# The last two of seven pair products deferred into the next stage, the experts' products all plain, and low parts computed on GpSimd

## The chip, the cores and the metric

One core of one Trainium2 chip runs the whole program in one launch. TensorE (PE) does the matmuls; PEld is its loading of weights. VectorE (DVE), ScalarE (ACT) and GpSimd (POOL) do elementwise work; SyncE (SP) and POOL issue DMAs. The metric is the device time of one execution in microseconds (us), a median over runs. Each engine works through its own list of instructions in order, and starts one when the semaphores that it names have been reached.

## The reference

Attention over 2 x 8 heads of 576 x 64, then a mixture of 8 experts, then a dense feed-forward, all float32. What bears on the change is the last two:

```
for e in range(E):                  # 8 experts, d_model 512, d_ff 1024
    h = np.maximum(x @ w1[e], 0.0)
    ye = h @ w2[e]
    out += P[:, e:e + 1] * ye       # P: balanced gates
...
h = x @ w_in                        # d_ff 2048
g = np.maximum(h, 0.0) + np.log1p(np.exp(-np.abs(h)))
return (g @ w_out).astype(np.float32)
```

x has 1152 rows (tokens) of 512.

## The kernel before

Each float32 operand is split into a high part (rounded to the matmul's format, by ACT) and a low part (the operand less its high part, by DVE or POOL); a product is three matmuls: high by high, high by low, low by high. In tile names the last letter, h or l, is that part.

The hidden dimension is worked off in 20 batches x of 512 features: 0 to 15 are the experts' (two each; relu), 16 to 19 the dense layer's (softplus). The rows are two halves g of 576. A batch has a first product (x by w1, tiles `ph`, L502), always as seven products of quarters; for a half g and each of two feature blocks a and b it is p1, p2, p6, p7, p5, p3, p4, six matmuls of 288 columns each, called a **first unit** here (a1, b1, ... b4: 14 to a half).

The second product (hidden by w2, added into `acc`) has two forms. The **plain** one (`downs`, L578) takes 36 **down units** of three matmuls of 512 columns to a batch. The **seven** form (`pairs`, L420), for the batches in `SEVEN` (14, 17, 18, 19), takes for each half seven products of quarters, a11·b11, s3·t3, s2·t2, a22·t4, s1·t1, s4·b22, a12·b21, each as two **pair units** r of six matmuls of 256 columns, and for the 128 rows left over (one row tile, NB) four down units. It has two PSUM banks, one for each r; each bank holds two halves of columns. A pair unit accumulates onto one half of a bank; behind every pair unit DVE adds that half into `acc` (`add_to`, L381; 128x256), and the next unit that accumulates on that half waits for the add.

For the seven form ACT writes the hidden block as plain words (`evict`, tile `hw`), and `h_steps` makes from them the sums s1 to s4 (POOL, L334), their high parts (ACT, L327) and low parts (DVE, L330). `prep_t` makes t1 to t4 from w2 (sums on POOL L256, high parts on ACT L243, low parts `tl` on DVE L245); `prep_b` splits w2's blocks (ACT L226, `w2l` on DVE L228). `prep1` sums and splits the next batch's w1 (POOL L161 to L170, ACT L152, DVE L155). POOL's chain has one scratch tile `xw` for both s and t.

Nothing is reordered by a scheduler: `play` reads a string. `a1` to `b4` issue a first unit, `d` the next second unit, and each such token then lets one step of each waiting helper (`back`, `side`, `bot`) be issued. A **first stage** of x plays the first units of half 1 of x with the second units of half 0; a **second stage** plays the first units of half 0 of x+1 with the second units of half 1; behind batch 19 comes a **last stage** without first units. `E` and `F` (and before `e`) start parts of `h_steps`, `x`/`y` start `prep_b`/`prep_t`.

Of the kernel before, what the change touches and what calls it, by code (L numbers as in the profile page):

```python
# [20 lines left out]
def attention_moe_ffn(ctx, tc, q, k, v, s, w_gate, w1, w2, w_in, w_out, out):  # L21
    nc = tc.nc
# [107 lines left out]
    SEVEN = (NX - 2, NX + 1, NX + 2, NX + 3)  # L130
# [89 lines left out]
    def prep_b(x, n):  # L220

        if x >= NH:
            return
        raw = blocks(x)[n]
        hi, lo = (w2_block(n, z) for z in w2_t)
        nc.scalar.activation(out=hi, in_=raw, func=AF.Copy)  # L226
        yield
        nc.vector.tensor_tensor(out=lo, in0=raw, in1=f(hi), op=ALU.subtract)  # L228
        if n == "21":
            load(x + 1, 2, 1)  # L230
        ready.add((x, "b" + n))
        yield
# [7 lines left out]
    def t_part(x, n, src, part):  # L240
# [3 lines left out]
        else:  # L244
            nc.vector.tensor_tensor(out=l, in0=src, in1=f(h), op=ALU.subtract)  # L245
# [76 lines left out]
    def h_steps(x, g, part):  # L322
# [13 lines left out]
        if part == "e":  # L336
            hold((x, g), (None,))
            sum_("s3", "a11", "a21", ALU.subtract)
            high("a11")
            yield  # L340
            low("a11")
            yield
            last = (x - 1 + g, 1 - g)
            assert not seven(last[0]) or (*last, "done") in ready
            high("s3")
            yield
        elif part == "E":
            high("m")
            high("a22")
            yield  # L350
            low("s3")
            low("m")
            low("a22")
            sum_("s2", "a22", "s3", ALU.subtract)
            yield
            sum_("s1", "a21", "a22", ALU.add)
            yield
            high("a12")
            yield
            low("a12")  # L360
            high("s2")
            yield
            sum_("s4", "a12", "s2", ALU.subtract)
            high("s1")
            yield
            low("s2")
            low("s1")
            hold(None, ((x, g),))
            yield
        else:  # L370
# [3 lines left out]
            yield  # L374

# [13 lines left out]
    def pairs(x, g, middle=None):  # L389
# [16 lines left out]
        for a, b, bank, start, tile_, col, first in (  # L406
# [4 lines left out]
            if a == "s3" and middle is not None:  # L411
                yield from middle
            for r in range(2):
# [9 lines left out]
                if a == "s4" and r:  # L423
                    ready.add((x, g, "done"))
# [61 lines left out]
    class Unit:  # L486
# [32 lines left out]
        def p2(self):  # L519
# [4 lines left out]
            evict(self.x, 5 if seven(self.x) else 0, b, self.p, self.h0)  # L524
# [11 lines left out]
        def p5(self):  # L536
# [5 lines left out]
            evict(self.x, 1, t, self.p + 2, self.h1)  # L542
# [60 lines left out]
    with tc.manual_schedule():  # L603
# [685 lines left out]
        def play(seq, todo, d=None):  # L1289


            for z in seq.split():
# [14 lines left out]
                if z[0] in "eEF":  # L1307
                    g = int(z[1])
                    if seven(x if g else x + (z[0] == "e")):
                        side.append(h_steps(x if g else x + (z[0] == "e"), g, z[0]))  # L1310
# [13 lines left out]
        A7_SEQ = "E0 a1 b1 a2 b2 =0 d d a6 d b6 d d F0 a7 d d b7 =1 d d a5 d b5 d d a3 d b3 e1 a4 d b4"  # L1324
        A7_LAST = "E0 a1 b1 a2 b2 d a6 d d b6 d d F0 a7 d d b7 d d a5 d b5 d a3 d b3 e1 a4 b4 d d"
        B7_SEQ = ("E1 a1 b1 =2 a2 b2 d d d d a6 d d {11} b6 d d {3} F1 a7 d b7 d {2} a5 d b5 d {4} d a3 d {1} d b3 e0 d {22} a4 d b4 d {21}")
        TO_SEVEN = B_SEQ.replace("b2", "b2 y3 y2 y4 y1").replace("b3", "b3 e0")
        B7 = {True: {"11": "x11 x12 y0", "3": "y3", "2": "y2", "4": "y4", "1": "y1", "22": "x22", "21": "x21"},
              False: {"11": "w0 w1", "3": "", "2": "", "4": "", "1": "", "22": "", "21": "w2 w3"}}
# [12 lines left out]
        for x in range(NH):  # L1342
# [8 lines left out]
            if seven(x):  # L1351
                play(A7_SEQ if x + 1 < NH else A7_LAST, products(x, 1), pairs(x, 0))
# [9 lines left out]
            if seven(x):  # L1362
                if x + 1 < NH:
                    seq = B7_SEQ
# [79 lines left out]
```

## Time and profile before

| | |
|---|---|
| median of 3 runs | 1088.13 us (1088.04 to 1088.27) |
| the profiled execution | 1089.59 us, of which 1087.8 are the span of the trace |
| mean granted TensorE clock | 0.996 |
| PE busy | 1056.2 us (97% of the span) |
| DVE, ACT, POOL busy | 799.5, 525.3, 406.1 us |

A busy PE is pipelined: a matmul's duration overlaps the next one's start, so the price of a unit is read from start to start. A gap before a matmul is printed in brackets with what ended it. Stretches are given in us from the start of the span. Batch 13 is plain (742.77 to 790.25), batch 14 seven (790.25 to 839.68); the stages of 17 to 19 go from 942.30 to 1084.15.

### The profile page before, as it was taken

The numbers are of one execution on the slowest core, as the hardware profiler recorded it, in microseconds if no ns is written. First come the engines' busy times: TensorE is split into PE (matmuls) and PEld (weight loads), VectorE is DVE, ScalarE is ACT, GpSimd is POOL, SyncE is SP. The second block draws the span as 40 slices with busy tenths as digits, with TensorE's granted clock in tenths as the row PEclk, the third lists the DMA queues.
The fourth block names the chain that finished last, engine by engine and source line by source line (L and its number), as shares of the span: only waits on it lengthen the run. The fifth ranks groups of instructions, "written<-read, shape, count | busy, mean of one in ns | idle before, by whom it ended". The sixth has DMA issues, their size and how long they took to land.

```text
span 1087.8 us, 18435 instructions
## 1 busy us (share of the span) xinstructions
PE 1056.2 (97%) x6876; PEld 942.5 (87%) x6876; DVE 799.5 (73%) x1725; ACT 525.3 (48%) x1232; POOL 406.1 (37%) x449
## 2 busy tenths in 40 slices
PE   6999999999999999999999999999999999999987
PEld 4777888889888888988888898888899888898987
DVE  5576566667877878787887888775477487678876
ACT  6998544334443433434343343334454365555542
POOL 8885303053342414134241423423262233546321
PEclk9999999999999999999999999999999999999999
DMA  6221111122232222223222231311111011201002
GB/s 195 78 83 55 39 40 39 40 92 96 89 130 88 80 97 98 100 77 124 91 74 98 97 107 68 127 59 39 39 40 59 20 40 39 78 21 59 1 16 73
DMA packets 31538, 78.47 MB, mean 72 GB/s; under 512 B 5856, under 2 KB 13024, under 8 KB 31448
## 3 DMA queue, kind: packets, MB, share of 16 engines
q1 hardware_dynamic: 28704, 68.69, 18.9%
q0 software_dynamic: 2560, 8.39, 2.0%
q8 instruction: 54, 0.88, 0.3%
q14 instruction: 36, 0.29, 0.1%
q10 hardware_dynamic: 184, 0.20, 0.1%
HBM read 65.99 MB, written 10.75 MB: 71 GB/s over the span
## 4 chain that ended last, share of the span: by engine, by line
PE 82%; DVE 10%; ACT 3%; issue 2%; POOL 2%; DMA 0%; POOLq 0%; ACTq 0%; DVEq 0%
PE py L578 36%; PE ph L502 35%; PE py L420 5%; DVE hl L330 2%; PE sc L794 2%; POOL eb L857 1%; PE pv L901 1%; DVE sl L330 1%; PE tr L875 1%; DVE xl L1198 1%; DVE acc L381 1%; DVE xt L1229 1%; DVE ph L523 1%; PE sc L798 1%; DVE w1l L155 1%
## 5 line engine op out<-in xcount | busy, mean ns | idle before, releaser
L502 PE MATMUL ph<-xh,w1h 128*128 128x288 f32 x1120 | 331.7, 296 | 0.3 <-ACT v L510 0.3
L502 PE MATMUL ph<-xh,w1l 128*128 128x288 f32 x1120 | 330.8, 295 | 0.0
L502 PE MATMUL ph<-xl,w1h 128*128 128x288 f32 x1120 | 329.3, 294 | 0.0
L578 PE MATMUL py<-w2h,hh 128*128 128x512 f32 x588 | 233.5, 397 | 1.0 <-DVE acc L590 1.0
L578 PE MATMUL py<-w2l,hh 128*128 128x512 f32 x588 | 232.5, 395 | 0.2 <-POOL w2l L201 0.2
L578 PE MATMUL py<-w2h,hl 128*128 128x512 f32 x588 | 232.4, 395 | 0.0
L502 PEld LDWEIGHTS ph<-xh,w1h 128*128 128x128 f32 x1120 | 210.0, 188 | 18.4 <-ACT v L510 0.5
L502 PEld LDWEIGHTS ph<-xl,w1h 128*128 128x128 f32 x1120 | 210.4, 188 | 16.9
L502 PEld LDWEIGHTS ph<-xh,w1l 128*128 128x128 f32 x1120 | 210.3, 188 | 0.0
L510 ACT ACTIVATE v<-ph 128x288 f32<-128x288 f32 x160 | 64.0, 409 | 187.5 <-PE ph L502 184.8
L469 ACT ACTIVATE hh<-ph 128x288 fp32r<-128x288 f32 x180 | 73.7, 411 | 151.8 <-DVE ph L552 78.2
L578 PEld LDWEIGHTS py<-w2h,hl 128*128 128x128 f32 x588 | 110.5, 188 | 26.5
L201 POOL TENSOR_TENSOR w2l<-raw,w2h 128x512 fp32r<-128x512 f32 x36 | 51.3, 1427 | 215.9 <-ACT w2h L199 215.9
L596 DVE SCALAR_TENSOR_TENSOR acc<-py,gate,acc 128x512 f32<-128x512 f32 x118 | 88.0, 746 | 49.2 <-PE py L578 49.0
L1166 POOL TENSOR_TENSOR cm<-cm,ct 128x512 f32<-128x512 f32 x32 | 45.1, 1408 | 201.5 <-DVE ct L1164 201.5
L578 PEld LDWEIGHTS py<-w2h,hh 128*128 128x128 f32 x588 | 110.4, 188 | 10.5 <-DVE acc L590 1.2
L578 PEld LDWEIGHTS py<-w2l,hh 128*128 128x128 f32 x588 | 110.5, 188 | 10.0 <-POOL w2l L201 0.7
L155 DVE TENSOR_TENSOR w1l<-raw,w1h 128x512 fp32r<-128x512 f32 (+1 forms) x160 | 109.8, 686 | 11.3 <-ACT w1h L152 11.3
L476 DVE SCALAR_TENSOR_TENSOR hl<-ph,hh 128x288 fp32r<-128x288 f32 x180 | 81.2, 453 | 26.7 <-ACT hh L469 25.1
L152 ACT ACTIVATE w1h<-raw 128x512 fp32r<-128x512 f32 (+1 forms) x160 | 91.1, 571 | 0.0
L541 DVE TENSOR_TENSOR t<-ph,v 128x288 f32<-128x288 f32 x80 | 36.4, 455 | 54.5 <-ACT v L510 53.9
L510 ACT ACTIVATE u<-ph 128x288 f32<-128x288 f32 x80 | 32.7, 411 | 55.5 <-PE ph L502 53.4
(246 smaller groups left out, 1779.2 us busy)
## 6 DMA issues: line engine op xcount, KB each, us to landing
raw<-in_w SPq DMA_DIRECT2D x64, 512.0 KB
f<-in_w_in SPq DMA_DIRECT2D x16, 512.0 KB
f<-in_w_out SPq DMA_DIRECT2D x16, 512.0 KB
wd<-cm POOLq DMA_DIRECT2D x32, 256.0 KB, 3.1
raw<-wd SPq DMA_DIRECT2D x16, 512.0 KB
vv<-in_v SPq DMA_DIRECT2D x8, 256.0 KB
out<-acc SPq DMA_DIRECT2D x16, 128.0 KB
qk<-in_k SPq DMA_DIRECT2D x7, 288.0 KB
```

Of the source, the lines that this page charges most:

```text
L152: nc.scalar.activation(out=hi[:, o], in_=t[:, src], func=AF.Copy)
L155: nc.vector.tensor_tensor(out=lo[:, o], in0=t[:, src], in1=f(hi[:, o]), op=ALU.subtract)
L201: (nc.gpsimd if i else nc.vector).tensor_tensor(out=lo, in0=t[:, r], in1=f(hi), op=ALU.subtract)
L420: nc.tensor.matmul(o, u, v, start=(start and c == 0 and n == 0), stop=(c == 1 and n == 2), skip_group_check=True)
L469: nc.scalar.activation(out=hh, in_=z, func=AF.Relu)
L476: nc.vector.scalar_tensor_tensor(out=hl, in0=z, scalar=0.0, in1=f(hh), op0=ALU.max, op1=ALU.subtract)
L502: nc.tensor.matmul(o, u, v, start=(start and c == 0 and n == 0), stop=(c == 1 and n == 2), skip_group_check=True)
L510: nc.scalar.activation(out=t, in_=self.a, func=AF.Copy)
L541: defer(0, lambda: nc.vector.tensor_tensor(out=t, in0=self.c, in1=u4, op=ALU.add))
L578: nc.tensor.matmul(py[t], u, v, start=(k == 0 and n == 0), stop=(k == NF - 1 and n == 2))
L596: nc.vector.scalar_tensor_tensor(out=a, in0=py, scalar=gate_t[0][:, t, e:e + 1], in1=a, op0=ALU.mult, op1=ALU.add)
L1166: nc.gpsimd.tensor_tensor(out=m, in0=m, in1=f(t), op=ALU.add)
```

## The change

Batch 14 leaves `SEVEN`. In the stages of 17 to 19, `h_steps` is no longer begun in the stage before (`e`): `E` holds all but s4. The generator `pairs` gives only its first five products (ten units) in its own stage; the last two (s4·b22 and a12·b21, four units) stay in `d` and are issued at the start of the next stage. The four down units of the tile NB move ahead of the second half's pairs, as before, but behind the deferred four; in the last stage they are played between these. In the first stage of 17, which has nothing deferred, the first pair unit comes behind a6. Of w2's blocks, b22 and b21 are split in the first stage (`X22`, `X21`), no longer in the second. The words of p2 and p5 are written 8 and 4 flushes later (before 5 and 1). The low parts `tl` and `w2l` in `t_part` and `prep_b` go from VectorE to GpSimd.

```
-    SEVEN = (NX - 2, NX + 1, NX + 2, NX + 3)
+    SEVEN = (NX + 1, NX + 2, NX + 3)
...
     def prep_b(x, n):
...
-        nc.vector.tensor_tensor(out=lo, in0=raw, in1=f(hi), op=ALU.subtract)
+        nc.gpsimd.tensor_tensor(out=lo, in0=raw, in1=f(hi), op=ALU.subtract)
...
     def t_part(x, n, src, part):
...
-            nc.vector.tensor_tensor(out=l, in0=src, in1=f(h), op=ALU.subtract)
+            nc.gpsimd.tensor_tensor(out=l, in0=src, in1=f(h), op=ALU.subtract)
...
     def h_steps(x, g, part):
...
-        if part == "e":
-            hold((x, g), (None,))
-            sum_("s3", "a11", "a21", ALU.subtract)
-            high("a11")
-            yield
-            low("a11")
-            yield
-            last = (x - 1 + g, 1 - g)
-            assert not seven(last[0]) or (*last, "done") in ready
-            high("s3")
-            yield
-        elif part == "E":
-            high("m")
-            high("a22")
-            yield
-            low("s3")
-            low("m")
-            low("a22")
-            sum_("s2", "a22", "s3", ALU.subtract)
-            yield
-            sum_("s1", "a21", "a22", ALU.add)
-            yield
-            high("a12")
-            yield
-            low("a12")
-            high("s2")
-            yield
-            sum_("s4", "a12", "s2", ALU.subtract)
-            high("s1")
-            yield
-            low("s2")
-            low("s1")
-            hold(None, ((x, g),))
-            yield
-        else:
+        if part == "F":
+            assert (x, g, "s3 done") in ready
+            return
+        hold((x, g), (None,))
+        sum_("s3", "a11", "a21", ALU.subtract)
+        high("m")
+        yield
+        high("a11")
+        low("m")
+        yield
+        high("a22")
+        low("a11")
+        yield
+        low("a22")
+        yield
+        last = (x - 1 + g, 1 - g)
+        assert not seven(last[0]) or (*last, "s4 done") in ready
+        high("s3")
+        yield
+        low("s3")
+        yield
+        sum_("s2", "a22", "s3", ALU.subtract)
+        yield
+        high("a12")
+        yield
+        sum_("s1", "a21", "a22", ALU.add)
+        yield
+        high("s2")
+        yield
+        low("s2")
+        yield
+        low("a12")
+        high("s1")
+        yield
+        sum_("s4", "a12", "s2", ALU.subtract)
+        low("s1")
+        hold(None, ((x, g),))
+        yield
...
     class Unit:
...
-            evict(self.x, 5 if seven(self.x) else 0, b, self.p, self.h0)
+            evict(self.x, 8 if seven(self.x) else 0, b, self.p, self.h0)
-            evict(self.x, 1, t, self.p + 2, self.h1)
+            evict(self.x, 4 if seven(self.x) else 1, t, self.p + 2, self.h1)
...
         def play(seq, todo, d=None):
...
-                if z[0] in "eEF":
-                    g = int(z[1])
-                    if seven(x if g else x + (z[0] == "e")):
-                        side.append(h_steps(x if g else x + (z[0] == "e"), g, z[0]))
+                if z[0] in "EF":
+                    side.append(h_steps(x, int(z[1]), z[0]))
+                    continue
+                if z[0] == "X":
+                    bot.append(prep_b(x, z[1:]))
...
-        A7_SEQ = "E0 a1 b1 a2 b2 =0 d d a6 d b6 d d F0 a7 d d b7 =1 d d a5 d b5 d d a3 d b3 e1 a4 d b4"
-        A7_LAST = "E0 a1 b1 a2 b2 d a6 d d b6 d d F0 a7 d d b7 d d a5 d b5 d a3 d b3 e1 a4 b4 d d"
-        B7_SEQ = ("E1 a1 b1 =2 a2 b2 d d d d a6 d d {11} b6 d d {3} F1 a7 d b7 d {2} a5 d b5 d {4} d a3 d {1} d b3 e0 d {22} a4 d b4 d {21}")
-        TO_SEVEN = B_SEQ.replace("b2", "b2 y3 y2 y4 y1").replace("b3", "b3 e0")
-        B7 = {True: {"11": "x11 x12 y0", "3": "y3", "2": "y2", "4": "y4", "1": "y1", "22": "x22", "21": "x21"},
-              False: {"11": "w0 w1", "3": "", "2": "", "4": "", "1": "", "22": "", "21": "w2 w3"}}
+        A7_SEQ = ("E0 a1 ~ b1 ~ {22} a2 ~ b2 ~ {21} =0 a6 d b6 d a7 d b7 d F0 =1 a5 d b5 d a3 d b3 d a4 d b4 d")
+        B7_SEQ = ("E1 a1 d b1 d a2 d b2 d =2 a6 d d b6 d d {12} a7 d d {11} b7 d d {3} F1 a5 d b5 d {2} a3 d b3 d {4} a4 d b4 d {1}")
+        TO_SEVEN = B_SEQ.replace("b2", "b2 y3 y2 y4 y1")
+        B7 = {True: {"12": "x12", "11": "x11 y0", "3": "y3", "2": "y2", "4": "y4", "1": "y1"},
+              False: {"12": "", "11": "w0 w1", "3": "", "2": "", "4": "", "1": "d d d d w2 w3"}}
+        A7 = {True: {"~": "d", "{22}": "X22", "{21}": "X21"}, False: {"~": "", "{22}": "", "{21}": ""}}
+        LAST = "E1 d d D d D d D D d d d d F1 " + "d " * 10
...
         for x in range(NH):
...
-                play(A7_SEQ if x + 1 < NH else A7_LAST, products(x, 1), pairs(x, 0))
+                seq = A7_SEQ
+                for k, z in A7[seven(x - 1)].items():
+                    seq = seq.replace(k, z)
+                d = then(d if seven(x - 1) else (), pairs(x, 0))
+                play(seq, products(x, 1), d)
...
+                    d = then(d, downs(x, [(NB,)]), pairs(x, 1))
-                    play(seq, products(x + 1, 0), then(downs(x, [(NB,)]), pairs(x, 1)))
+                    play(seq, products(x + 1, 0), d)
-                    play("E1 n n n n " + "d " * 8 + "F1 " + "d " * 10, {}, pairs(x, 1, downs(x, [(NB,)], "tr")))
+                    middle = downs(x, [(NB,)], "tr")
+                    play(LAST, {"D": lambda: next(middle)}, then(d, pairs(x, 1)))
```

In `pairs` and `h_steps` the flag "done" is now kept for each product ("s3 done", "s4 done").

VectorE at the opening of the first stage of batch 18, before (`sl` and `hl` are low parts of s and of the hidden quarters, `acc` an add behind a pair unit, `ph` an add of the first product):

```order
L381 TENSOR_TENSOR acc<-py,acc 128x256
L330 TENSOR_TENSOR sl<-xw,sh 128x512
L330 TENSOR_TENSOR hl<-hw,hh 128x4x64
L330 TENSOR_TENSOR hl<-hw,hh 128x2x2x128
L228 TENSOR_TENSOR w2l<-raw_10292,w2h 128x2x256
L523 TENSOR_TENSOR ph<-ph,v 128x288 x2
L381 TENSOR_TENSOR acc<-py,acc 128x256
L330 TENSOR_TENSOR hl<-hw,hh 128x2x2x128
L381 TENSOR_TENSOR acc<-py,acc 128x256
L330 TENSOR_TENSOR sl<-xw,sh 128x512
L330 TENSOR_TENSOR hl<-hw,hh 128x2x2x128
L381 TENSOR_TENSOR acc<-py,acc 128x256 x3
```

and after (L384 is L381 of before, L524 is L523):

```order
L330 TENSOR_TENSOR hl<-hw,hh 128x4x64
L330 TENSOR_TENSOR hl<-hw,hh 128x2x2x128
L384 TENSOR_TENSOR acc<-py,acc 128x256
L330 TENSOR_TENSOR hl<-hw,hh 128x2x2x128
L524 TENSOR_TENSOR ph<-ph,v 128x288
L384 TENSOR_TENSOR acc<-py,acc 128x256
L330 TENSOR_TENSOR sl<-xw,sh 128x512
L524 TENSOR_TENSOR ph<-ph,v 128x288
L384 TENSOR_TENSOR acc<-py,acc 128x256 x2
L330 TENSOR_TENSOR sl<-xw,sh 128x512
L384 TENSOR_TENSOR acc<-py,acc 128x256
L330 TENSOR_TENSOR hl<-hw,hh 128x2x2x128 x2
```

The `w2l` is gone. All low parts of the half but s4's now stand in this stage, mostly one between two adds; before, a11's stood in the stage ahead, and s3's, m's and a22's followed each other.

GpSimd in the same stage, before, from the sum for t2 on (`xw<-hw` is s3, `xw<-hw,xw` s2, `hw<-hw` s1, `hw<-hw,xw` s4, `raw` with 128x256 the sums of w1):

```order
L256 TENSOR_TENSOR xw<-raw_10292,raw_10267 128x512
L256 TENSOR_TENSOR xw<-raw_10292,xw 128x512
L334 TENSOR_TENSOR xw<-hw 128x512
L334 TENSOR_TENSOR xw<-hw,xw 128x512
L334 TENSOR_TENSOR hw<-hw 128x2x2x128
L161 TENSOR_TENSOR raw_10624<-raw_10624 128x256
L163 TENSOR_TENSOR raw_10624<-raw_10624 128x256
L334 TENSOR_TENSOR hw<-hw,xw 128x2x2x128
L161 TENSOR_TENSOR raw_10681<-raw_10681 128x256
```

and after, from the low part of t4 on:

```order
L245 TENSOR_TENSOR tl<-xw,th 128x512
L334 TENSOR_TENSOR xw<-hw 128x512
L245 TENSOR_TENSOR tl<-raw_10129,th 128x512
L228 TENSOR_TENSOR w2l<-raw_10154,w2h 128x2x256
L334 TENSOR_TENSOR xw<-hw,xw 128x512
L161 TENSOR_TENSOR raw_10505<-raw_10505 128x256
L334 TENSOR_TENSOR hw<-hw 128x2x2x128
L163 TENSOR_TENSOR raw_10505<-raw_10505 128x256
L228 TENSOR_TENSOR w2l<-raw_10154,w2h 128x2x256
L161 TENSOR_TENSOR raw_10565<-raw_10565 128x256
L163 TENSOR_TENSOR raw_10565<-raw_10565 128x256
L334 TENSOR_TENSOR hw<-hw,xw 128x2x2x128
```

Three low parts, one `tl` and two `w2l`, now stand between s3, s2, s1 and s4, and s4 has all four first sums of w1 ahead of it.

ScalarE in the same stage around s4's high part (`v` is the copy of p5 that the next product on its PSUM tile waits for, `hw` a word of the hidden block), before:

```order
L152 ACTIVATE w1h_10931<-raw_10624 128x512
L458 ACTIVATE hw<-ph 128x288
L152 ACTIVATE w1h_10957<-raw_10681 128x512
L327 ACTIVATE sh<-hw 128x512
L510 ACTIVATE v<-ph 128x288
L152 ACTIVATE w1h_11019<-raw_10624 128x512
L458 ACTIVATE hw<-t_11009 128x288
L510 ACTIVATE v<-ph 128x288
```

and after:

```order
L152 ACTIVATE w1h_10823<-raw_10565 128x512
L511 ACTIVATE v<-ph 128x288
L327 ACTIVATE sh<-hw 128x512
L511 ACTIVATE v<-ph 128x288
L459 ACTIVATE hw<-ph 128x288
L459 ACTIVATE hw<-t_10834 128x288
L459 ACTIVATE hw<-ph 128x288
L152 ACTIVATE w1h_10889<-raw_10505 128x512
L459 ACTIVATE hw<-t_10854 128x288
```

The high part of s4 stands between the copies of a5 and of b5; before, both came behind it.

## Rows read from the trace of the kernel before

**Rows 1.** The page: busy time of each engine, and the chain that ended last.
```profile
PE 1056.2 (97%) x6876; PEld 942.5 (87%) x6876; DVE 799.5 (73%) x1725; ACT 525.3 (48%) x1232; POOL 406.1 (37%) x449
...
PE 82%; DVE 10%; ACT 3%; issue 2%; POOL 2%; DMA 0%; POOLq 0%; ACTq 0%; DVEq 0%
```

**Rows 2.** Stages: length, busy us (count) by engine, granted clock, DMA share, GB/s.
```profile
742.77:790.25 47.48, 47.48 (x279) 42.56 (x277) 25.05 (x47) 18.84 (x45) 15.26 (x15) 1.00 0.13 45
790.25:839.68 49.43, 45.68 (x350) 44.52 (x349) 39.68 (x75) 25.46 (x56) 18.60 (x16) 1.00 0.16 54
942.30:965.61 23.31, 21.55 (x170) 21.14 (x169) 18.36 (x34) 12.80 (x29) 14.70 (x13) 1.00 0.14 46
965.61:993.03 27.42, 24.80 (x182) 23.46 (x181) 23.73 (x39) 15.13 (x34) 11.13 (x8) 1.00 0.11 39
993.03:1015.87 22.84, 21.53 (x170) 21.12 (x169) 18.41 (x36) 12.05 (x28) 13.27 (x12) 1.00 0.14 48
1015.87:1043.29 27.42, 24.78 (x182) 23.47 (x181) 23.74 (x39) 15.15 (x34) 11.13 (x8) 1.00 0.00 1
1043.29:1066.33 23.04, 21.54 (x170) 21.11 (x168) 16.04 (x32) 10.52 (x25) 5.53 (x4) 1.00 0.10 35
1066.33:1084.15 17.82, 15.27 (x98) 14.10 (x96) 13.43 (x23) 3.46 (x7) 3.98 (x3) 0.90 0.20 68
```

**Rows 3.** TensorE in order of time: start, duration, line, tiles; first matmuls of units.
```profile
640.43 0.29 PE L502 MATMUL ph<-xh,w1h 128*128 128x288 f32 x1
...
641.23 0.39 PE L578 MATMUL py<-w2h,hh 128*128 128x512 f32 x1
...
641.93 0.39 PE L578 MATMUL py<-w2h,hh 128*128 128x512 f32 x1
...
954.39 0.28 PE L420 MATMUL py<-th,hh 128*128 128x256 f32 x1
...
955.10 0.29 PE L502 MATMUL ph<-xh,w1h 128*128 128x288 f32 x1
```

**Rows 4.** TensorE's waits in the stages with pairs (in brackets).
```profile
823.24 0.38 PE L420 MATMUL py<-w2h,hh 128*128 128x256 f32 x1 [1.69 <-DVE acc L596]
...
974.61 0.39 PE L420 MATMUL py<-w2h,hh 128*128 128x256 f32 x1 [1.34 <-DVE acc L593]
...
985.52 0.38 PE L420 MATMUL py<-th,hh 128*128 128x256 f32 x1 [1.08 <-DVE acc L381]
...
1075.16 0.36 PE L420 MATMUL py<-th,sh 128*128 128x256 f32 x1 [2.23 <-DVE acc L381]
```

**Rows 5.** VectorE and then GpSimd ahead of the wait at 974.61.
```profile
971.58 0.68 DVE L330 TENSOR_TENSOR sl<-xw,sh 128x512 fp32r<-128x512 f32 x1
972.18 1.78 DVE L330 TENSOR_TENSOR hl<-hw,hh 128x512 fp32r<-128x512 f32 x1
973.88 0.68 DVE L593 TENSOR_TENSOR acc<-py,acc 128x512 f32<-128x512 f32 x1
...
971.73 1.67 POOL L334 TENSOR_TENSOR hw<-hw,xw 128x512 f32<-128x512 f32 x1 [0.96 <-DVE hl L330]
```

**Rows 6.** Groups from 930 to 1065: busy us, mean ns; idle before, and what ended it.
```profile
L381 DVE TENSOR_TENSOR acc<-py,acc 128x256 f32<-128x256 f32 x68 | 27.9, 417 | 11.7 <-PE py L420 11.3
L334 POOL TENSOR_TENSOR hw<-hw,xw 128x512 f32<-128x512 f32 x5 | 8.1, 1616 | 2.6 <-DVE hl L330 2.6
L245 DVE TENSOR_TENSOR tl<-xw,th 128x512 fp32r<-128x512 f32 x7 | 4.8, 687 | 3.2 <-ACT th L243 3.2
L256 POOL TENSOR_TENSOR xw<-raw,xw 128x512 f32<-128x512 f32 x3 | 3.9, 1298 | 8.5 <-DVE tl L245 8.5
L161 POOL TENSOR_TENSOR raw<-raw 128x256 f32<-128x256 f32 x4 | 3.9, 963 | 0.0
```

**Rows 7.** The clock in the last stage, in the columns of the stages.
```profile
1076.70:1080.10 3.40, 3.40 (x18) 3.40 (x17) 1.87 (x4) 0.00 (x0) 0.00 (x0) 0.50 0.11 39
```

**Rows 8.** ScalarE in the second stage of batch 17: a wait for a POOL sum.
```profile
982.56 0.64 ACT L243 ACTIVATE th<-raw 128x512 fp32r<-128x512 f32 x1 [3.65 <-POOL raw L256]
```

More of the change, by code (lines that the diff above doesn't have):

```diff
@@ L387, in add_to, with pairs @@
             nc.sync.dma_start(out=out[t * P:(t + 1) * P, cols], in_=a)
-    def pairs(x, g, middle=None):
+    def pairs(x, g):
         z = h_sets(g)
@@ L410, in pairs @@
                 ("a12", "b21", 1, True, 0, 0, False)):
-            if a == "s3" and middle is not None:
-                yield from middle
             for r in range(2):
@@ L422, in pairs @@
                 flush()
-                if a == "s4" and r:
-                    ready.add((x, g, "done"))
+                if r:
+                    ready.add((x, g, a + " done"))
                 add_to(x, rows_of(g) // P + 2 * r + tile_, d[col], o, first, (tile_, col))
```

## The prediction, made before the changed kernel was run

> **What bounds it now.** I read the page first: PE is busy for 97% of the span and holds 82% of the chain that ended last [rows 1], so the time is PE's work plus PE's waits. The table by stages then tells where the waits are. Batch 13, plain, is 47.48 us long and PE is busy for all of it; the stages with pairs are not full [rows 2]. From start to start a first unit costs 0.80 us (640.43 to 641.23), a down unit 0.70 (to 641.93), a pair unit 0.71 (954.39 to 955.10) [rows 3]. So a plain batch is 28 x 0.80 + 36 x 0.70 = 47.6, as measured. A first stage with pairs would be 14 x 0.80 + 14 x 0.71 = 21.14, a second 14 x 0.80 + 14 x 0.71 + 4 x 0.70 = 23.94, the last 14 x 0.71 + 4 x 0.70 = 12.74. Measured in batches 17 to 19 [rows 2]: 23.31, 27.42, 22.84, 27.42, 23.04, 17.82; over the ideal by 2.17, 3.48, 1.70, 3.48, 1.90 and 5.08, together **17.8 us lost**.
>
> The waits printed before matmuls show what the loss is: nearly always a unit that waits for a DVE add [rows 4]. Ahead of the one at 974.61 DVE does two low parts and only then the add of NB's total, and the second of them takes 1.78 us, because POOL has a sum running from 971.73 to 973.40 [rows 5]; the one ahead of it took 0.68. An add that reads PSUM is not stretched: 417 ns on average [rows 6]. In the last stage two waits of DVE adds end with one of 2.23 us [rows 4], after which the granted clock is 0.5, the 1.2 GHz level, for 3.4 us [rows 7]: half of that, 1.7, is lost again.
>
> **Batch 14.** It had 49.43 us; as a plain batch it should take what batch 13 takes, 47.48 [rows 2]. By parts: 36 x 0.70 - 28 x 0.71 - 4 x 0.70 = 2.5 us more matmul work, against 49.43 - 45.08 = 4.35 us of waits, such as the 1.69 at 823.24 [rows 4]. Gain **1.95**. The cover is PE's own work: DVE is busy for 25.05 of 47.48 us, ACT for 18.84, POOL for 15.26, so the plain form's `hl` and `w2l` are hidden. Without that cover the waits would stay in another form and the batch lose 2.5.
>
> **Batches 17 to 19, PE's work.** The ten or four units only move: the six stages become 18.3, 23.94, 21.14, 23.94, 21.14 and 15.58, again 124.0 in all. What changes is the waits, which I follow by the order of each engine, with the durations DVE 0.69 for a low part and 0.42 for an add, POOL 1.30, or 1.62 where DVE is in its way, 0.96 for a 256-column sum [rows 6], ACT 0.64 for a high part [rows 8].
>
> Behind a pair unit the same bank half is wanted next after 5 us in a first stage (a first unit stands between any two pair units) and after 2.3 us across a stage's border, where it was 0.7 to 2.2. A single low part caught behind POOL (1.78) no longer delays PE there. What remains late:
>
> First stage of 17: nothing is deferred into it, s3 has 7 us; 0.3 us left of 2.17, with bounds 0 and 1.
>
> Second stages (two): the total of NB is still behind the low parts of s2, a12 and s1 on DVE, and a11's second unit waits for its bank. From the stage's start: s3's low part ends at 5.9, POOL's s2 at 7.2, ACT's high part at 8.4 (behind a6's copy and a piece of w1), POOL's s1 holds DVE up until 8.9, the low part of s2 ends at 9.6, a12's at 10.3, POOL's s4 then holds s1's low part up to 12.15, the total ends at 12.85. The bank is wanted at 11.95 (6 first units, 4 pair units, 4 down units, a7 and one pair unit). So 1.0 of wait, where it was 1.34 and a slow restart. The later waits (1.08 at 985.52) go: the high part of t3 still waits for a POOL sum on ACT [rows 8] and holds the copy of b5, but only b3 wants it, 0.3 us too late. 1.3 per stage, bounds 0.3 and 3.48 as before.
>
> First stage of 18: POOL now does in the second stage before it two `w2l`, two sums, then t3, t2, t4, each as sum, ACT's high part, low part: from about 12 us on without a rest, and reaches s3 some 3 us into the first stage. ACT has the high parts of t4 and t1 ahead of a11's and a22's, DVE has a22's low part ahead of the add of a12's first unit: it ends at 7.4, the bank is wanted at 6.7, 0.85 us of wait with the second unit's. Behind that POOL has the rest of the eight low parts and the first sums of w1 ahead of s4, which ends at about 18.2; ACT waits with s4's high part and has b5's copy behind it, done at 19.2, while b3 is due at 17.9: 1.3. Together 2.1; bounds 0.3 and 5 (one more late POOL sum of 1.62 on each of the two places).
>
> First stage of 19: no next w1, eight POOL sums less, so only 0.85; bounds 0 and 1.9.
>
> Last stage: 22 units without first units, 15.58. The first down unit waits 0.55 for m's low part, s2's first unit 0.4 for its low part, s4's first unit 0.8 for the add of s1, since the low part of s4 stands ahead of it on DVE; 0.1 elsewhere: 1.85. The longest is 0.8, not 2.23, so I count no fall of the clock. Bounds 0.5 and 5.08.
>
> Sum of waits 0.3 + 2 x 1.3 + 2.1 + 0.85 + 1.85 = 7.7, and 1.5 (an estimate, about a tenth of the present loss) for short ones. 17.8 - 9.2 = **8.6 gained**. With batch 14: 10.55. Span 1087.8 - 10.55 = 1077.25. The profiled execution took 1089.59, 1.8 more than its span; the median of the runs, 1088.13, is 0.33 above that span. So **1077.5** for the median.
>
> **The low parts themselves.** Twenty go from DVE (0.69 each [rows 6]) to POOL (1.30 to 1.62): DVE is relieved of 14 us, POOL gets 26 to 32 more. In one second and one first stage POOL was busy for 11.1 and 13.3 of 50 us [rows 2]; with eight more it is 35 to 38 of some 47. That is why I let s4 be late and not the t's, which have 10 us and more.
>
> **Rivals.** (1) Nearly all waits go: POOL's operations fall between DVE's, and only some 2.5 us stay: 1088.1 - 1.95 - 15.3 = 1070.9. For it: 5 us between an add and its use. Against: the order of DVE at the total of NB hardly changes.
>
> (2) Only the ends gain: the middle four stages lose what they lost (10.6), first stage of 17 and last stage gain 1.9 and 3.2, batch 14 1.95: 1081.1. With one POOL delay more per stage pair 1083. For it: DVE is busy for 42 of 50 us in a pair of stages [rows 2], and each low part that is left can still be held by a POOL operation that is now more often there.
>
> (3) POOL becomes the bound, and it is slower. Its 20 operations of 512 columns at 1.73 (a sum of 1.30 and DVE's 0.43 in front) and 8 sums at about 1 make 43 us, and its waits for ACT's high parts, eight of 0.64, 5 more; if s3 to s4 of the second stage then start late too, another 6: 54 per pair of stages against 50.3 now, 4 more in each of two, and the other stages as they were. With batch 14's and 3 from the end that would be 1088.1 + 8 - 1.95 - 3 = 1091. It decides once POOL has no idle time in a second stage ahead of b12's low part. Against: the chain above leaves it about 5 us there. The Trainium skill speaks for this rival: "SBUF — State Buffer", section "SBUF: two separate sides", says that a DVE operation with two SBUF inputs and a GpSimd operation that reads SBUF exclude each other for a whole instruction. The trace agrees: the 1.78 us low part ends 0.56 after POOL's sum does [rows 5]. By that rule moving a low part frees 0.68 of the shared ports and takes 1.30, so it adds contention.
>
> (4) It does nothing, or nearly: the waits only change places, 1084 to 1090.
>
> **Chances.** Forecast 0.55 (1073.5 to 1081), rival 1 0.15, rival 2 0.17 (to 1084), rival 3 0.06, rival 4 0.07. The range 1071 to 1084 leaves out rival 3, most of 4 and half of 1. A measurement of this kernel tells 0.2%, 2.2 us, from no change: faster than 1085.9 is the forecast, rivals 1 and 2 and a third of 4, 0.89; the same 0.04; slower 0.07.
>
> **What would show it.** Right: batch 14 about 47.5 us with PE full; no half clock at the end; in the second stages one wait of about 1 us before a11's second unit; in the first stage of 18 waits at the first new pair unit and at b3, the latter behind ACT's wait for a POOL sum; less in that of 19. Wrong: waits of over 1.5 us before adds in several stages, or POOL without idle time through a whole pair of stages (rival 3); no wait at NB's total (rival 1).

## The result and the profile after

The changed kernel takes 1078.80 us (median; 1078.66 to 1079.17) against 1088.09 (1087.96 to 1088.27): 9.3 us less, a ratio of 0.9915 [0.9898, 0.9932]. Predicted were 1077.5, between 1071 and 1084.

The page of the changed kernel, engines and chain, against [rows 1]:

```profile
PE 1056.1 (98%) x6804; PEld 938.2 (87%) x6804; DVE 769.4 (71%) x1681; ACT 514.5 (48%) x1212; POOL 415.2 (39%) x457
...
PE 88%; DVE 5%; ACT 3%; POOL 2%; issue 1%; DMA 0%; POOLq 0%; ACTq 0%; DVEq 0%; SPq 0%
```

PE's busy time is the same as before to 0.1 us, the span is 10.9 us shorter (1087.8 to 1076.9), and half of DVE's share of the chain is gone: what went is time in which PE stood. The two spans overstate it. In the profiled execution of before the clock fell to its lower level for 3.4 us near the start, in work that the change does not touch, and batch 14 begins 1.65 us later there (790.25 against 788.60). Such a fall is in 5 of the 13 profiled executions of this document, of kernels of either order. Before, then after, columns as in [rows 2]:

```profile
18.60:22.00 3.40, 3.40 (x18) 2.58 (x20) 0.60 (x5) 3.04 (x10) 3.40 (x5) 0.50 0.98 374
```
```profile
18.60:22.00 3.40, 3.38 (x32) 2.38 (x30) 1.45 (x9) 3.28 (x9) 3.40 (x5) 1.00 1.01 372
```

The stages after, against [rows 2]: batch 14, then first and second stages of 17 and 18, first of 19, last:

```profile
788.60:836.08 47.48, 47.48 (x279) 42.56 (x278) 24.24 (x49) 18.76 (x42) 8.42 (x10) 1.00 0.14 45
938.71:958.56 19.85, 19.03 (x146) 18.39 (x145) 16.29 (x28) 11.26 (x27) 16.03 (x14) 1.00 0.16 54
958.56:983.21 24.65, 24.09 (x183) 23.35 (x181) 18.75 (x35) 13.12 (x30) 13.77 (x11) 1.00 0.12 44
983.21:1007.50 24.29, 22.29 (x171) 21.21 (x170) 19.99 (x31) 13.48 (x30) 21.41 (x18) 1.00 0.13 44
1007.50:1032.14 24.64, 24.10 (x182) 23.34 (x181) 18.77 (x35) 13.12 (x30) 13.77 (x11) 1.00 0.00 1
1032.14:1054.86 22.72, 21.77 (x170) 21.13 (x169) 15.99 (x28) 11.52 (x26) 14.23 (x10) 1.00 0.04 13
1054.86:1073.25 18.39, 16.96 (x122) 15.45 (x120) 13.53 (x27) 4.81 (x9) 3.87 (x3) 1.00 0.27 93
```

The time that a stage loses is its length less its ideal as the prediction gives it (for the changed kernel 18.3, 23.94, 21.14, 23.94, 21.14, 15.58). Lost time by stage, in us:

| stage | before | predicted | after |
|---|---|---|---|
| first, 17 | 2.17 | 0.3 | 1.55 |
| second, 17 | 3.48 | 1.3 | 0.71 |
| first, 18 | 1.70 | 2.1 | 3.15 |
| second, 18 | 3.48 | 1.3 | 0.70 |
| first, 19 | 1.90 | 0.85 | 1.58 |
| last | 5.08 | 1.85 | 2.81 |
| short waits, not placed | – | 1.5 | (above) |
| sum | 17.8 | 9.2 | 10.5 |

So 7.3 come from the pairs, and batch 14 gave 49.43 - 47.48 = 1.95: together 9.25, and with the 1.65 from the start the 10.9 of the spans. That 9.25 is so near the 9.3 of the medians is chance. The granted clock is 1.00 to the end now, where [rows 7] had 3.4 us of half clock; that fall, 1.7 of the last stage's gain, is not in every execution of the old order (kernel 1 below has the long wait without it). Among the executions of before that were timed beside the experiments, the three with a mean granted clock of 1.000 took 1086.86 to 1087.20 us, and all nine of the changed kernel, at the same clock, 1078.66 to 1079.17: at a like clock the change gives about 8 us, near the 7.55 that 9.25 less 1.7 leaves.

TensorE's longest waits after in four of the stages (in brackets), against [rows 4]: a11's second unit in the second stage of 17, a11's first and s2's first unit in the first of 18, a22's second unit in the last stage:

```profile
971.16 0.38 PE L421 MATMUL py<-w2h,hh 128*128 128x256 f32 x1 [0.56 <-DVE acc L594]
...
990.72 0.36 PE L421 MATMUL py<-w2h,hh 128*128 128x256 f32 x1 [0.39 <-DVE acc L384]
...
998.74 0.36 PE L421 MATMUL py<-th,sh 128*128 128x256 f32 x1 [1.16 <-DVE acc L384]
...
1067.98 0.38 PE L421 MATMUL py<-th,hh 128*128 128x256 f32 x1 [1.01 <-DVE acc L384]
```

What stands ahead of three of them on DVE, and beside it on POOL (after, in order of time by engine; against [rows 5]):

```profile
969.24 1.27 DVE L330 TENSOR_TENSOR hl<-hw,hh 128x512 fp32r<-128x512 f32 x1 [0.72 <-ACT hh L327]
970.43 0.68 DVE L594 TENSOR_TENSOR acc<-py,acc 128x512 f32<-128x512 f32 x1
...
995.68 2.58 DVE L330 TENSOR_TENSOR hl<-hw,hh 128x512 fp32r<-128x512 f32 x2
998.18 0.41 DVE L384 TENSOR_TENSOR acc<-py,acc 128x256 f32<-128x256 f32 x1
...
1065.87 1.72 DVE L330 TENSOR_TENSOR hl<-hw,hh 128x512 fp32r<-128x512 f32 x1
1067.52 0.74 DVE L384 TENSOR_TENSOR acc<-py,acc 128x256 f32<-128x256 f32 x2
...
968.66 1.30 POOL L334 TENSOR_TENSOR hw<-hw,xw 128x512 f32<-128x512 f32 x1 [1.63 <-DVE hl L330]
...
995.97 1.74 POOL L228 TENSOR_TENSOR w2l<-raw,w2h 128x512 fp32r<-128x512 f32 x1
...
1065.76 1.29 POOL L334 TENSOR_TENSOR hw<-hw,xw 128x512 f32<-128x512 f32 x1 [1.99 <-DVE hl L330]
```

Each time it is the pattern of before: a low part held up by a POOL operation, then the add that PE waits for. At 995.97 the POOL operation is a moved low part, `w2l`.

### The profile page after: what moved, and what is told of

It is laid out like the page before. It is cut to its first block, busy times and chain, and to the rows that moved or that the text cites. A ratio compares the mean times of both kernels' runs of the same rounds, so it can differ in the third digit from the quotient of the medians.

```text
span 1076.9 us, 18212 instructions
## 1 busy us (share of the span) xinstructions
PE 1056.1 (98%) x6804; PEld 938.2 (87%) x6804; DVE 769.4 (71%) x1681; ACT 514.5 (48%) x1212; POOL 415.2 (39%) x457
## 4 chain that ended last, share of the span: by engine, by line
PE 88%; DVE 5%; ACT 3%; POOL 2%; issue 1%; DMA 0%; POOLq 0%; ACTq 0%; DVEq 0%; SPq 0%
PE py L579 39%; PE ph L503 38%; PE py L421 4%; PE sc L795 1%; PE pv L902 1%; DVE xl L1199 1%; DVE hl L330 1%; PE tr L876 1%; ACT eb L845 1%; POOL eb L858 1%; DVE xt L1230 1%; PE sc L799 0%; DVE acc L384 0%; ACT pt L890 0%; PE tr L870 0%
## 5 line engine op out<-in xcount | busy, mean ns | idle before, releaser
L579 PE MATMUL py<-w2h,hh 128*128 128x512 f32 x620 | 246.2, 397 | 1.0 <-DVE acc L591 1.0
L579 PE MATMUL py<-w2l,hh 128*128 128x512 f32 x620 | 245.1, 395 | 0.2 <-POOL w2l L201 0.2
L579 PE MATMUL py<-w2h,hl 128*128 128x512 f32 x620 | 245.1, 395 | 0.0
L470 ACT ACTIVATE hh<-ph 128x288 fp32r<-128x288 f32 x192 | 78.6, 411 | 159.8 <-DVE ph L553 80.8
L579 PEld LDWEIGHTS py<-w2h,hl 128*128 128x128 f32 x620 | 116.5, 188 | 28.0
L597 DVE SCALAR_TENSOR_TENSOR acc<-py,gate,acc 128x512 f32<-128x512 f32 x126 | 93.9, 745 | 56.2 <-PE py L579 56.0
L579 PEld LDWEIGHTS py<-w2h,hh 128*128 128x128 f32 x620 | 116.4, 188 | 10.8 <-DVE acc L591 1.2
L579 PEld LDWEIGHTS py<-w2l,hh 128*128 128x128 f32 x620 | 116.6, 188 | 10.3 <-POOL w2l L201 0.7
L477 DVE SCALAR_TENSOR_TENSOR hl<-ph,hh 128x288 fp32r<-128x288 f32 x192 | 86.4, 452 | 31.2 <-ACT hh L470 29.5
```

The lines of the kernel that those rows point to most:

```text
L470: nc.scalar.activation(out=hh, in_=z, func=AF.Relu)
L477: nc.vector.scalar_tensor_tensor(out=hl, in0=z, scalar=0.0, in1=f(hh), op0=ALU.max, op1=ALU.subtract)
L579: nc.tensor.matmul(py[t], u, v, start=(k == 0 and n == 0), stop=(k == NF - 1 and n == 2))
L597: nc.vector.scalar_tensor_tensor(out=a, in0=py, scalar=gate_t[0][:, t, e:e + 1], in1=a, op0=ALU.mult, op1=ALU.add)
```

## The experiments

They were timed in three sets, each beside the kernel before on the set's chip (it took 1088.1 to 1088.8 us). The kernels are called 1 to 10 by the headings; of two in one heading the expectation that stands first is that of the first. The changed kernel itself, run once more in one of the sets, took 1078.97 us and showed the same waits (0.55, 0.40, 1.16, 1.01). Medians that differ by about 1 us need care here: an execution with a mean granted clock of 0.998 took 0.8 to 1.4 us more than one of the same kernel at 1.0, the changed kernel had 1.0 in all nine, and most of kernels 1 to 10 had executions of both kinds.

> The changed kernel itself on this chip, for the comparisons of this set: 1078.8 us; first stage 18 with 2.0 us of waits at its pair units, both second stages with 0.55 us before a11's second unit, the last with 1.0 us before a22's second unit.

**1 and 2. Batch 14 alone.** Before with batch 14 plain, and, with the edit turned round, after with batch 14 in seven products:

```
-    SEVEN = (NX - 2, NX + 1, NX + 2, NX + 3)
+    SEVEN = (NX + 1, NX + 2, NX + 3)
```

> The kernel before with batch 14 plain and nothing else changed. If the gain of that part is the difference of the two forms of one batch (49.43 against 47.48 us in the trace of before), the time is 1088.1 - 1.95 = 1086.2 us, and the stages of 17 to 19 lose what they lost, 17.8 us. Rival: batch 14's waits were only the bill for late low parts that another batch pays instead, then 1087.5 to 1088.5.

Measured 1085.87 us, ratio 0.9977 [0.9968, 0.9987]. The stage:

```profile
789.59:837.07 47.48, 47.48 (x279) 42.56 (x278) 24.23 (x49) 18.75 (x42) 8.43 (x10) 1.00 0.13 45
```

> The kernel after with batch 14 as seven pair products again, in the new order. If a batch with deferral loses what 17 loses now (1.55 + 0.71 us), batch 14 takes 45.08 + 2.3 = 47.4 us against 47.48 plain: 1078.3 to 1079.3 us, no difference. Rival: without a next seven batch the four deferred units are played in a row at the end of its second stage and its adds, which multiply by the gate, are slower: 1080 to 1081.5.

Measured 1079.25 us, ratio 0.9914 [0.9901, 0.9928]:

```profile
788.67:836.46 47.79, 46.21 (x351) 44.74 (x349) 39.81 (x77) 25.15 (x58) 19.89 (x17) 1.00 0.17 56
```

Plain is worth 1.95 us under the old order (by the stages; the medians mix executions with and without falls of the clock), and 0.3 under the new one, where PE stands for only 1.58 us in the seven products of batch 14 (49.43 - 45.68 = 3.75 before). The two parts overlap: with batch 14 left in seven products, the new order alone gives all of the 9.3 us but some 0.3.

**3 and 4. Where the low parts run, without and with the deferral.** Lines 228 and 245, VectorE to GpSimd in before, and back in after:

```
-        nc.vector.tensor_tensor(out=lo, in0=raw, in1=f(hi), op=ALU.subtract)
+        nc.gpsimd.tensor_tensor(out=lo, in0=raw, in1=f(hi), op=ALU.subtract)
...
-            nc.vector.tensor_tensor(out=l, in0=src, in1=f(h), op=ALU.subtract)
+            nc.gpsimd.tensor_tensor(out=l, in0=src, in1=f(h), op=ALU.subtract)
```

> The kernel before with the low parts of t and of w2's blocks on GpSimd and nothing else changed (batch 14 as seven). Theory A (VectorE's load is what the adds wait for): 1084 to 1086.5 us. Theory B (VectorE's waits behind GpSimd are): 1087.5 to 1090.

Measured 1095.07 us, ratio 1.0061 [1.0048, 1.0073]: 6.2 us slower, which neither theory allowed. In its second stage of batch 17 (line 228 on POOL, then 256; ACT; DVE; PE):

```profile
978.86 2.99 POOL L228 TENSOR_TENSOR w2l<-raw,w2h 128x512 fp32r<-128x512 f32 x2 [4.53 <-ACT w2h L226]
981.81 1.74 POOL L256 TENSOR_TENSOR raw<-raw 128x512 f32<-128x512 f32 x1
983.62 1.28 POOL L256 TENSOR_TENSOR raw<-raw,raw 128x512 f32<-128x512 f32 x1
...
984.94 0.63 ACT L243 ACTIVATE th<-raw 128x512 fp32r<-128x512 f32 x1 [5.12 <-POOL raw L256]
985.48 0.39 ACT L510 ACTIVATE v<-ph 128x288 f32<-128x288 f32 x1
...
985.90 0.46 DVE L541 TENSOR_TENSOR t<-ph,v 128x288 f32<-128x288 f32 x1 [3.17 <-ACT v L510]
986.27 0.41 DVE L381 TENSOR_TENSOR acc<-py,acc 128x256 f32<-128x256 f32 x1
...
986.74 0.38 PE L420 MATMUL py<-th,hh 128*128 128x256 f32 x1 [2.02 <-DVE acc L381]
```

This is read downwards: two low parts of 1.5 us put POOL's sums back, ACT stands 5.12 us with a high part of such a sum (3.65 in [rows 8]), the copy of b5 behind it is late, DVE stands 3.17 us with b5's add, and the pair unit's add behind that makes PE wait 2.02 (1.08 in [rows 4]). It is the prediction's third rival in its effect, late sums, but not in its reason, a POOL without idle time: POOL stood 4.53 us just ahead of the two low parts. Part of the 6.2 is TensorE's clock, which in the last two stages fell twice in this profile (granted 0.93 and 0.91 on average, where [rows 2] has 1.00 and 0.90).

> The kernel after with all moved low parts back on VectorE: deferral and batch 14 alone. Theory A, the move to GpSimd carries a good part, since VectorE has 20 low parts of 0.68 us more between the adds that TensorE waits for: 1081 to 1084 us. Theory B, the deferral carries it and GpSimd only trades VectorE's own time for waits behind GpSimd's operations: 1077.5 to 1079.5.

Measured 1078.35 us, ratio 0.9906 [0.9893, 0.992], no slower than after. With the deferral the move gives nothing, and by the trace it costs a little: the six stages take 133.75 us here and 134.54 after. (Two of the four executions had a clock of 0.998, 1078.74 and 1078.88; the others took 1077.96.) By stage the difference is large (second of 17, first of 18; then DVE, POOL and the wait in the second of 17):

```profile
959.73:985.77 26.04, 24.57 (x183) 23.45 (x181) 21.41 (x39) 13.44 (x31) 9.77 (x7) 1.00 0.12 42
985.77:1007.75 21.98, 21.51 (x171) 21.07 (x169) 19.75 (x35) 12.97 (x30) 15.44 (x13) 1.00 0.14 49
```
```profile
979.65 1.55 DVE L245 TENSOR_TENSOR tl<-raw,th 128x512 fp32r<-128x512 f32 x1
...
978.91 1.73 POOL L256 TENSOR_TENSOR xw<-raw,raw 128x512 f32<-128x512 f32 x1
...
981.95 0.39 PE L421 MATMUL py<-th,hh 128*128 128x256 f32 x1 [0.92 <-DVE acc L384]
```

The second stage is 1.39 longer than after (24.65), the first 2.31 shorter (24.29).

**5 and 6. The two moves apart.** After, with only `w2l` or only `tl` back on VectorE.

> The changed kernel with one of its two moves to GpSimd undone: the low parts of w2's own blocks (w2l, line 228) run on VectorE again, those of the sums (tl, line 245) stay on GpSimd. Theory (a pair unit waits for the sum of the unit before it on the same PSUM bank, and a VectorE low part that runs beside a GpSimd operation holds that sum up): the waits of first stage 18 that stand behind w2l on GpSimd (0.39 us at a11's second unit, 1.16 at s2's second, 0.21 and 0.24 after them, 2.0 together) shrink to about 0.5 as in the kernel with all low parts on VectorE, and the 0.92 us that that kernel lost in each second stage behind tl on VectorE does not come back: 1078.8 less 1.5 is 1077.3 us. Rival (the low parts only change places, whichever engine has them): 1078.4 us, as with all of them on VectorE, with a new wait of 0.7 us or more in each second stage.

Measured 1078.80 us, ratio 0.9912 [0.9898, 0.9925]; the two executions with a clock of 1.0 took 1078.14 and 1078.22, some 0.8 less than the changed kernel. Second of 17 and first of 18, then the wait of s2 in the latter (it is s2's first unit, and the 0.39 a11's first, though the expectation says second):

```profile
958.68:983.57 24.89, 24.32 (x183) 23.43 (x181) 19.48 (x37) 13.06 (x30) 10.90 (x9) 1.00 0.13 44
983.57:1007.18 23.61, 22.26 (x170) 21.16 (x169) 19.93 (x33) 13.38 (x30) 19.42 (x16) 1.00 0.13 46
```
```profile
998.41 0.35 PE L421 MATMUL py<-th,sh 128*128 128x256 f32 x1 [0.66 <-DVE acc L384]
```

The wait behind `w2l` fell from 1.16 to 0.66, not to nothing, and each second stage took 0.24 more for the low parts now on DVE: the theory has the places right and the size too large; the rival's new wait of 0.7 is not there.

> The changed kernel with the other of its two moves undone: the low parts of the sums (tl, line 245) run on VectorE again, those of w2's own blocks (w2l, line 228) stay on GpSimd. It completes the four ways to place the two. Theory (a low part costs where it meets an operation of the other engine on the path of a pair unit's sum, so the price of a placement goes by stage and not by the number of instructions): second stages as with all of them on VectorE, 26.0 us against 24.65 (tl on VectorE beside GpSimd's sums), first stage 18 in between, about 23 us against 24.3, since the 1.16 us behind w2l stay and only tl's part of the wait goes, first stage 19 about 21 against 22.2: 1078.9 + 2.7 - 1.3 - 1.2 is about 1079 us. Rival (the effects of the two moves add up, -0.5 for both undone and -0.2 for w2l alone): 1078.6 us, with the second stages at 24.65.

Measured 1077.94 us, ratio 0.9907 [0.9892, 0.9922]:

```profile
958.78:984.48 25.70, 24.32 (x182) 23.35 (x181) 20.76 (x37) 13.43 (x31) 12.57 (x9) 1.00 0.13 42
984.48:1007.17 22.69, 21.51 (x171) 21.08 (x169) 19.80 (x33) 13.11 (x30) 17.23 (x15) 1.00 0.15 48
```

The stages came as the theory put them (26.0 and 23 were expected), its sum was 1 us too high. `tl` on VectorE lengthens the second stage by 1.05 and shortens the first one behind it by 1.60. Not all of the latter need be won in the first stage itself (kernel 10 puts 0.5 there): while PE loses time in a second stage, the other engines can get ahead with what the next stage needs.

**7. Is the wait for the bank or for the column half?** After, with four banks in the last stage. The first unit on a bank has to start a new sum there, so s3's does:

```
+        last = x == NH - 1 and g == 1
...
+            if last:
+                py.append([ps.tile([P, DM], F32, tag="sc", name="ph", bufs=4) for _ in range(2)])
+                continue
...
-                o = py[r][:, d[bank]]
+                o = py[r][bank][:, :HW] if last else py[r][:, d[bank]]
...
-  start=(start and c == 0 and n == 0)
+  start=((start or last and a == "s3") and c == 0 and n == 0)
```

> The changed kernel with one edit: in the last stage each of the four halves of the pair products' accumulators has a PSUM bank of its own (the four that the first products no longer use), in place of two halves in each of two banks. Order of instructions and their number stay. Theory (a unit waits for the sum on the other half of its bank): the 1.01 us before a22's second unit in the last stage goes, since the sum it waits for, s2's second unit, lies in another bank now, and its own bank's sum (s3's second unit) ended 3 us earlier: last stage 17.4 instead of 18.4 us, 1077.8 us. Rival (it waits for its operands or for the sum on its own column half, and the trace only lists the last releaser): the wait stays at 1.0 us and the time at 1078.8 us.

Measured 1078.60 us, ratio 0.9910 [0.9896, 0.9924], in its median no clear difference to after; its two executions with a clock of 0.999 and 1.0 took 1077.95 and 1078.10, some 0.9 less. The trace is clear. DVE and PE in the last stage (1066.69 is the first matmul of a22's second unit), then the stage:

```profile
1065.83 1.73 DVE L330 TENSOR_TENSOR hl<-hw,hh 128x512 fp32r<-128x512 f32 x1
1067.48 0.74 DVE L384 TENSOR_TENSOR acc<-ph,acc 128x256 f32<-128x256 f32 x2
...
1066.69 0.28 PE L425 MATMUL ph<-th,hh 128*128 128x256 f32 x1
...
1069.63 0.36 PE L425 MATMUL ph<-w2h,sh 128*128 128x256 f32 x1 [0.58 <-DVE acc L384]
```
```profile
1054.95:1072.70 17.75, 16.62 (x122) 15.12 (x120) 13.26 (x27) 4.81 (x9) 3.88 (x3) 1.00 0.29 97
```

The low part at 1065.83 is as long as ever, and a22's second unit starts 0.8 us before the add that it waited for has begun (1067.48): the 1.01 us were not those of its own half. Each half is now a tile as well as a bank of its own, and no run puts two tiles into one bank; which of the two makes the wait is not told apart, and "bank" below stands for both. Of the 1.01 0.74 come back, 0.58 at s4's first unit, which waits for the add on its own half behind the same DVE queue, and 0.16 for a low part. The stage is still 0.8 shorter (18.58 to 17.75), the rest from units that no longer stop a little at each add. The changed kernel's trace has the same in the other stages: of 72 pair units none starts less than 0.05 us after the end of the add of the last unit on its bank, and 19 start within 0.2. In 16 of the 19 that last unit is on the other half, and the add on their own half, where there was one, is at least 1.5 us old.

**8. The order ahead of NB's total.** Kernel 5, with the low part of s1 four steps later:

```
         sum_("s4", "a12", "s2", ALU.subtract)
+        if g and x + 1 < NH:
+            for _ in range(4):
+                yield
         low("s1")
```

> As the kernel with w2l on VectorE, and one more edit: in the second stages of batches 17 and 18 the low part of s1 (1.2 us on VectorE beside GpSimd's s4) stands four steps later, behind NB's total and the first two sums, where nothing waits for it for 5 us. Theory (the queue of VectorE ahead of the total sets the wait before a11's second unit): the 0.55 us at that unit goes in both second stages, 1.1 us less than the kernel with w2l on VectorE, about 1076.2 us. Rival (the wait is handed on: the sum of a11's first unit stands behind w1's low part, so the first unit of s3 waits instead): 0.4 us of wait at s3's first unit in both stages and no more than 0.3 us less.

Measured 1077.18 us, ratio 0.9897 [0.9883, 0.9910], 1.6 less than kernel 5. The second stages, and the total, which now waits for PE instead:

```profile
958.77:982.82 24.05, 24.05 (x182) 23.36 (x181) 18.98 (x37) 13.07 (x30) 10.89 (x9) 1.00 0.14 45
1006.43:1030.49 24.06, 24.06 (x182) 23.37 (x181) 19.00 (x37) 13.06 (x30) 10.90 (x9) 1.00 0.00 1
```
```profile
969.36 0.69 DVE L597 TENSOR_TENSOR acc<-py,acc 128x512 f32<-128x512 f32 x1 [0.63 <-PE py L582]
```

PE is busy for the whole stage, 0.1 above the ideal. No work has gone: one instruction in each stage stands elsewhere. The rival is out.

**9 and 10. Together.** First the edits of 5, 7 and 8; then also `tl` by stage:

```
-            nc.gpsimd.tensor_tensor(out=l, in0=src, in1=f(h), op=ALU.subtract)
+            (nc.vector if n in (1, 4) else nc.gpsimd).tensor_tensor(out=l, in0=src, in1=f(h), op=ALU.subtract)
```

> Three edits together, each of which was seen by itself: w2l on VectorE, s1's low part behind NB's total and the first two sums, four banks in the last stage. Theory (they act in different stages and add up): the stages of the kernel with the first two (24.05 and 24.06 us second stages, 23.6 first stage 18, 21.8 first stage 19) and the last stage of 18.3 us: 1077.18 - 0.82 is 1076.4 us. Rival (the last stage's gain shows in the trace alone, since the ends there are modelled and the last output still goes out at the same time): 1077.2 us.

Measured 1076.27 us, ratio 0.9890 [0.9875, 0.9904]: the edits add up, and the last stage's 0.8 shows in the runs here.

> The kernel with those three edits, and the low parts of the sums (tl) placed by stage: the two that fall into a first stage (t4, t1) on VectorE, the two of a second stage (t3, t2) on GpSimd. Theory (price by stage): first stage 18 and first stage 19 as with all low parts on VectorE, 22.0 and 20.5 us instead of 23.6 and 21.8, second stages still 24.05, last 18.3: 1076.4 - 1.6 - 1.3 is 1073.5 us. Rival (the waits in the first stages come from s1's and s2's low parts beside GpSimd's sums, not from tl there): first stages 23.6 and 21.8 as before, 1076.4 us.

Measured 1075.98 us (1075.77 to 1076.29), ratio 0.9888 [0.9871, 0.9904], the fastest of all, 2.8 under the changed kernel. First of 18 and first of 19:

```profile
983.81:1006.90 23.09, 21.96 (x170) 21.12 (x169) 20.22 (x35) 13.26 (x30) 16.39 (x14) 1.00 0.14 47
...
1030.95:1052.79 21.84, 21.61 (x171) 21.14 (x169) 16.71 (x32) 11.42 (x27) 8.56 (x6) 1.00 0.04 14
```

Each came 0.5 shorter than in kernel 8 (23.61, 22.37), where 1.6 and 1.3 were expected. So 0.5 us of each first stage were `tl`'s. s2's first unit still waits 0.66, as in kernel 5, behind low parts of the hidden block beside POOL's sums, which is the rival's reading, though no run singled out which low part it is. The mark for 22.0 and 20.5 was kernel 4, and there the second stage ahead is 2 us longer (26.04 for 24.05), so its first stages could not simply be added to kernel 9's second ones.

## Why the prediction was right, point by point

**Bound and direction: right.** PE's busy time did not change, the loss was waits for DVE adds behind held-up low parts, and the new order has fewer of them. Kernel 4 shows that the new order, with batch 14, carries the whole gain. No run takes the deferral apart from what came with it (low parts one by one between adds, the words of p2 and p5 later, b22 and b21 split elsewhere); that the room between add and use is what the deferral gives is argued.

**Batch 14: right**, 1.95 of 1.95 (kernel 1), though not as a gain of its own: under the new order it is worth 0.3 (kernel 2).

**The room behind a unit: the step that failed.** "Behind a pair unit the same bank half is wanted next after 5 us in a first stage": true of the half, but the wait is for the bank, and the other half is written in between. From a unit's end to the next start on its bank the trace of after mostly has 2.1 us where a first unit stands between any two pair units, 1.35 where pair units follow each other in twos, and 0.55 in the last stage. The first is more than the 0.7 that the prediction gives for the tightest places of before; all are less than one held-up low part and what queues behind it. Kernel 7 shows that this makes the wait in the last stage, the 0.05 us above speak for the other stages. The Trainium skill has the rule, which the prediction did not weigh: "PSUM — Partial Sum Buffer", section "PSUM bank collisions raise a hardware error", says that the compiler's scheduler puts a dependency between any two instructions of different engines that touch one bank in the same partitions, and that another address in the bank does not help. The trace agrees, by the 0.05 us above. With it, "a single low part caught behind POOL no longer delays PE there" falls: the three first stages and the last lost 1.25, 1.05, 0.73 and 0.96 us more than they were given. In the first of 19 the waits are 0.39 at a11's first and 0.56 at s2's first unit, where 0.85 was given for the former; the profile puts the 0.56 down to ACT, but the unit starts 0.15 after the add on its bank, as in the first of 18.

**First stage of 18: sum too small, the wait at b3 not there.** 2.1 were predicted, of them 1.3 at b3, behind ACT waiting for s4. The chain up to b3 came as predicted: POOL ends s4 18.0 us into the stage (18.2 predicted), ACT waits for it, and b5's copy is done at 19.0 (19.2). But PE had lost 1.8 us at pair units by then, so b3, which was due at 17.9, starts at 19.3 and is not held. The larger waits ahead of b3 covered this one. POOL, ACT and PE of the changed kernel:

```profile
999.95 1.29 POOL L334 TENSOR_TENSOR hw<-hw,xw 128x512 f32<-128x512 f32 x1
...
1001.27 0.63 ACT L327 ACTIVATE sh<-hw 128x512 fp32r<-128x512 f32 x1 [3.24 <-POOL hw L334]
1001.81 0.39 ACT L511 ACTIVATE v<-ph 128x288 f32<-128x288 f32 x1
...
1002.52 0.29 PE L503 MATMUL ph<-xh,w1h 128*128 128x288 f32 x1
```

The 3.15 us lost are at pair units instead: 1.16 at s2's first, behind a moved `w2l` (shown by kernel 5 for 0.5 of it), 0.39 at a11's first, where 0.85 was predicted, and short ones.

**Second stages: place right, size too large.** The wait at a11's second unit came as predicted, 0.56 in place of 1.0, and nothing at b3: 0.7 in place of 1.3. Kernel 8 removed it by the order, as the prediction's chain has it (the total stands behind s1's low part).

**Last stage: no half clock, as predicted; 2.81 lost for 1.85.** One wait of 1.01, at a22's second unit where 0.8 was set for s4's first: again the bank. The wait for m's low part came as 0.39 (0.55 predicted).

**The low parts: half right.** They do not pay: kernels 3 and 4 put the move at +6.2 us without the deferral and at nothing gained with it. The prediction counted 14 us less on DVE as relief, but a low part of 0.68 that DVE keeps takes 1.72 beside a POOL operation of 1.29 (1065.87). The Trainium skill, "SBUF — State Buffer", section "SBUF: two separate sides", which the prediction named for its third rival, says that of a DVE operation with two SBUF inputs and a GpSimd operation that reads SBUF, the one that starts first keeps the other out until it is done. The trace agrees: the low part ends 0.54 us after POOL's sum.

Errors of both signs (second stages 1.2 too much together, first and last stages 4.0 too little, 1.5 set aside for short waits) left the sum of the waits 1.3 us too small; that it is no more is in part luck. So is the path from there to the median. The span that the prediction started from held the fall of the clock near the start (1.65), which it did not see, so the span came out at 1076.9 for 1077.25; and for the same reason the 0.33 that it put between span and median is 1.9 in the changed kernel (1078.80 - 1076.9).

## What to carry to other kernels

Two accumulators in the halves of one PSUM bank (one tile) were one buffer for waits here: count the room between an add and the next matmul on the whole bank. Before work is moved to a less busy engine, look for what its queue already holds for others, and for the operations on the other engine that it will hold up; where it pays can differ from stage to stage. And a queue is often cured by its order: one low part moved behind the sum that is waited for gave 1.6 us in two stages, where moving twenty to another engine gave nothing.

## What had not been expected of the hardware

The granted clock fell to 0.5, the lower level, for some 3 us near the start (17 to 22 us) in 5 of 13 profiled executions, of the old order (before, kernels 1 and 3) and the new one (kernels 4 and 10) alike. It cost about 0.9 to 1.6 us: the first second-product matmul starts at 122.5 to 123.1 us in these five and at 121.5 to 121.7 in the other eight. Kernel 10's profile has it, kernel 9's does not, so their spans are level (1074.0 and 1073.9) though kernel 10's stages are 1.0 shorter. Nor does a long wait settle it: the 2.23 us in [rows 4] were followed by half clock, while kernel 1, with 2.22 us at the same unit, kept 1.00 to its end (the wait, then the stretch that has the units behind it):

```profile
1072.56 0.36 PE L420 MATMUL py<-th,sh 128*128 128x256 f32 x1 [2.22 <-DVE acc L381]
...
1072.00:1079.00 7.00, 6.39 (x49) 6.15 (x50) 4.22 (x11) 0.00 (x0) 0.00 (x0) 1.00 0.30 106
```
